# Recurrent attention and a gated FFN on one core: the order of the chunks and the size of the input transfers

## The chip, the cores and the metric

The kernel runs on one core of one Trainium2 chip. The core has a matrix engine (TensorE, PE in the profile), a vector engine (DVE), an activation engine (ACT), GpSimd (POOL) and SyncE (SP), which issues most transfers; 16 DMA engines move data between device memory and the on-chip SBUF. Matrix products are written to eight PSUM banks. The metric is the device time of one execution in microseconds (us).

## The reference

Inputs q, k, v and f_logit are float32 of shape (4 batches, 8 heads, 768 tokens, 48). Each head carries a 48 x 48 state from token to token:

```python
f = 1.0 / (1.0 + np.exp(-f_logit))
for t in range(S):
    state = f[:, :, t, :, None] * state + np.einsum('bhd,bhe->bhde', k[:, :, t], v[:, :, t])
    y[:, :, t] = np.einsum('bhd,bhde->bhe', q[:, :, t], state)
```

The eight heads of a token are then laid side by side to a row x of 384 values, batch after batch (3072 rows), and go through a gated FFN of width 1536:

```python
gate = np.maximum(x @ w_gate, 0.0)
val = x @ w_val
out = gate * val @ w_out
```

## The kernel before

**Chunks.** A batch of 768 tokens is cut into six chunks of 128, called steps (c = 0 to 5). Within a chunk the recurrence is matrix work. With b the running sum of log f, the kernel forms "hats": k times exp(-b) and q times exp(b). Products of hats, masked by a triangle, are the scores; scores times v plus q-hat times the old state is the output y; k-hat times v, added to the old state and scaled by the chunk's whole decay, is the new state. So a chunk of a batch needs the state of the chunk before it in that batch, and different batches do not depend on each other.

**Order.** The kernel goes step by step: step c of all four batches (512 tokens, one group), then step c + 1. The FFN of a group follows once the four chunks of x are there. For steps 0 and 1 the FFN's hidden part is begun in halves of two batches (`groups`).

**One chunk, by engine.** ACT computes exp and ln of the gate (`f_in`, `bneg`). TensorE sums them with a triangular matrix (cum, L715, L718). ACT takes both exponentials (`expo`). GpSimd multiplies them with k and q (`hats`, L737 and L740) and copies v to a padded layout (`vpad`, L772). The hats must be turned round so that the feature lies on partitions (`qkT`): for step 2 on TensorE (L751, copied by DVE in L756), for steps 3 to 5 by a transposing DMA issued on SyncE (L759). TensorE makes the scores (L780), DVE masks them (`ptm`, L785), TensorE makes y, and ACT copies it out. For steps 0 to 2 y is made in transposed form (L807) and copied straight to `xT`; for steps 3 to 5 it is made in natural form (L813, L817), copied to `xn` and turned by a transposing DMA (L832). The state is made by TensorE (L841), DVE (L544: plus old state) and GpSimd (L546: times decay).

**Steps 0 and 1 are loaded otherwise.** `load_duo` puts two neighbouring tokens in one partition (one run of 384 bytes in device memory) and two batches in the two halves of the partitions; `attention_duo` computes both batches of a pair at once from this layout, with its own masks (`seen`, `later`) and sums (`upto`, `below`, `halves`). From step 2 on `load` (L466) brings one step of a pair of batches with one token in a partition: 2048 runs of 192 bytes, 393 KB.

**FFN.** For each of 12 blocks of 128 hidden units `ffn_hidden` makes gate and value (L865, 3 + 3 matmuls of 512 columns), ACT the relu (L871), DVE the product (`gT`, L875). `ffn_out` makes 12 matmuls of 384 columns for each 128 tokens (L888); ACT copies the result (L898), SyncE stores it (L902). The weights are cast to bf16 on the way in, by DMAs issued on GpSimd (L486), in three pieces each (wg, wv, wo).

**The planner.** The whole program is a list of operations with engine, estimated duration, the tiles read and written and a priority. `Plan.schedule` runs a list scheduler over it with these estimates, and so fixes each engine's order of instructions and the PSUM banks; of operations that can start at the same time the one with the lower priority number goes first. At run time each engine works its list in order and waits on semaphores. FFN operations have a priority 1000 higher in number than attention, and `chain` keeps operations of one kind in order. Loads wait until the load `flight` before them has landed. `first` is the order of the first loads; `wg0@q0.1` means that piece 0 of wg waits until that load of q has landed. The planner's model of the DMA queue blocks the issuing engine while more than 3300 descriptors are pending (`CAP`). Until `warm_until` idle gaps of TensorE are filled with matmuls of zeros, and one PSUM bank is kept for them.

Of the kernel before, what the change touches and what calls it, by code (L numbers as in the profile page):

```python
# [93 lines left out]
class Plan:  # L94
# [15 lines left out]
    def link(self):  # L110
        writers, readers = {}, {}
        for op in self.ops:
# [3 lines left out]
            for d in op.follows:  # L116
                deps[d] = "order"
# [167 lines left out]
def bass_hgrn2_outer__then__ffn_reglu_kernel(  # L285
# [25 lines left out]
    GT = B * C  # L311
    assert S % C == 0 and HD == DM == 384 and H == 8 and D == 48 and GT == 512
# [12 lines left out]
    hats = sb("hats", [128, NH, 2, H, 64], BF16)  # L325
    NQ = 8
    qkT = sb("qkT", [128, NQ, 2, NP, C], BF16)
    NM = 4
    ptm_all = sb("ptm", [128, NM, 2, NP, C], BF16)
    ptm = [ptm_all[:, i] for i in range(NM)]  # L330
    NV = 4
    vpad = [sb(f"vpad{i}", [128, VW], BF16) for i in range(NV)]
    st = [[sb(f"st{b}_{i}", [128, SW], BF16) for i in range(2)] for b in range(B)]
    NA = 3
    dec = [sb(f"dec{i}", [128, B, NP, 2], F32) for i in range(NA)]
    NN = 3
    xn = [sb(f"xn{i}", [128, HD], BF16) for i in range(NN)]
    NS = 3
# [8 lines left out]
    NR = 4  # L347
    relu = [sb(f"relu{i}", [128, GT], BF16) for i in range(NR)]
    NO = 4
    osb = [sb(f"osb{i}", [128, DM], F32) for i in range(NO)]  # L350
    tri = sb("tri", [128, C], BF16)
    upto = sb("upto", [128, C], BF16)
    below = sb("below", [128, C], BF16)
    halves = sb("halves", [128, 2], BF16)
    seen = [sb(f"seen{i}", [128, C], BF16) for i in range(2)]
    later = [sb(f"later{i}", [128, C], BF16) for i in range(2)]
# [13 lines left out]
    PE_L = 0.30  # L370

    def act_t(n):
        return dict(occ=0.17 + n / 1150.0, lat=0.2)

    def dve_t(n):
        return dict(occ=0.14 + n / 950.0, lat=0.2)

    def pool_t(n):
        return dict(occ=0.15 + n * 2.2 / 1000.0, lat=0.2)

    def pool_c(n):
        return dict(occ=0.12 + n * 1.05 / 1000.0, lat=0.2)
# [4 lines left out]
    def fill(eng, name, ap, value, cols, prio, key=None):  # L387
        e = engine[eng]
        add(eng, lambda: e.memset(ap, value), [], [key or name], occ=0.1 + cols / 2000.0, prio=prio)

    def triangle(t, name, base, prio, step=-1):
# [46 lines left out]
    def slot_of(n, c, pr):  # L438
        return (2 * c + pr) % NL[n]

# [595 lines left out]
```

## Time and profile before

| | |
|---|---|
| timed runs | 212.6 and 213.74 us, median 213.17 |
| profiled execution, span | 212.9 us; the page shows no time outside it |
| TensorE busy | 193.7 us (91%), mean granted clock 0.984 |
| DVE, ACT, POOL busy | 108.6, 108.7, 81.5 us |
| queue q1 (SyncE's transfers) | 104064 packets, 27.93 MB, 62.4% of 16 engines' span |
| queue q0 (weights, from GpSimd) | 3984 packets, 3.54 MB, 10.1% |
| chain that ended last | PE 66%, DMA 18%, SP's queue 8% |
| issue to landing, median | qkT transpose 4.4 us, xT transpose 3.1 us, weight pieces 8.9 to 10.6 us |

A busy share is a mean over the span; the page also cuts the span into 40 slices of 5.32 us and gives each engine's busy tenths in each. The chain follows the work back from the last instruction, at every step to what released it. In the tables of windows each row is a stretch of the span: its length, busy time of each engine with the number of instructions, the granted TensorE clock, the busy share of the DMA engines (over 1 where packets overlap) and GB/s.

### The profile page before, as it was taken

The numbers are of one execution on the slowest core, as the hardware profiler recorded it, in microseconds if no ns is written. First come the engines' busy times: TensorE is split into PE (matmuls) and PEld (weight loads), VectorE is DVE, ScalarE is ACT, GpSimd is POOL, SyncE is SP. The second block draws the span as 40 slices with busy tenths as digits, with TensorE's granted clock in tenths as the row PEclk, the third lists the DMA queues.
The fourth block names the chain that finished last, engine by engine and source line by source line (L and its number), as shares of the span: only waits on it lengthen the run. The fifth ranks groups of instructions, "written<-read, shape, count | busy, mean of one in ns | idle before, by whom it ended". The sixth has DMA issues, their size and how long they took to land.

```text
span 212.9 us, 4759 instructions
## 1 busy us (share of the span) xinstructions
PE 193.7 (91%) x1929; PEld 109.7 (51%) x1949; DVE 108.6 (51%) x184; ACT 108.7 (51%) x235; POOL 81.5 (38%) x121
## 2 busy tenths in 40 slices
PE   7788599999998999997878999688999999999994
PEld 2265375466776764553433555253555444445562
DVE  7975564582189795664534473253533333233310
ACT  2663167444885878784372654644243344433411
POOL 8939217431795957774515453044000000000000
PEclk9999799999999999999996999999999999999999
DMA  5999999995899899996898995899222100011012
GB/s 125 242 236 220 225 205 220 216 237 121 178 237 210 179 188 189 167 226 133 191 183 183 203 221 125 150 223 150 61 50 64 37 37 37 37 39 38 37 39 109
DMA packets 108069, 31.76 MB, mean 149 GB/s; under 512 B 101136, under 2 KB 108048, under 8 KB 108048
## 3 DMA queue, kind: packets, MB, share of 16 engines
q1 hardware_dynamic: 104064, 27.93, 62.4%
q0 software_dynamic: 3984, 3.54, 10.1%
q8 instruction: 15, 0.25, 0.5%
q14 instruction: 6, 0.05, 0.1%
HBM read 25.95 MB, written 4.72 MB: 144 GB/s over the span
## 4 chain that ended last, share of the span: by engine, by line
PE 66%; DMA 18%; SPq 8%; ACT 2%; POOL 2%; issue 2%; DVE 1%
PE ps L865 37%; PE ps L888 18%; DMA qkT<-hats 5%; DMA wv<-in_moe_w_val_dram 4%; SPq L454 3%; DMA xT<-xn 3%; SPq L832 2%; DMA q_in<-in_q_dram 2%; SPq L759 2%; DMA k_in<-in_k_dram 2%; DMA f_in<-in_f_logit_dram 2%; PE ps L780 2%; PE ps L618 1%; PE ps L715 1%; PE ps L646 1%
## 5 line engine op out<-in xcount | busy, mean ns | idle before, releaser
L875 DVE TENSOR_TENSOR gT<-relu,ps 128x512 bf16<-128x512 bf16 (+1 forms) x82 | 50.2, 620 | 57.9 <-PE ps L865 51.1
L871 ACT ACTIVATE relu<-ps 128x512 bf16<-128x512 f32 (+1 forms) x82 | 44.5, 545 | 37.5 <-PE ps L865 34.3
L865 PE MATMUL ps<-xT,wv 128*128 128x512 bf16 (+1 forms) x243 | 61.1, 361 | 2.3 <-DMA wv<-in_moe_w_val_dram 2.2
L865 PE MATMUL ps<-xT,wg 128*128 128x512 bf16 (+1 forms) x231 | 58.8, 360 | 1.4 <-DMA wg<-in_moe_w_gate_dram 0.4
L888 PE MATMUL ps<-wo,gT 128*128 128x384 bf16 x288 | 51.3, 326 | 0.0
L888 PEld LDWEIGHTS ps<-wo,gT 128*128 128x128 bf16 x288 | 27.1, 98 | 19.2 <-issue 0.2
L865 PEld LDWEIGHTS ps<-xT,wv 128*128 128x128 bf16 x246 | 23.5, 100 | 24.0 <-DMA wv<-in_moe_w_val_dram 2.5
L865 PEld LDWEIGHTS ps<-xT,wg 128*128 128x128 bf16 x246 | 23.1, 100 | 20.4 <-issue 0.8
L898 ACT ACTIVATE osb<-ps 128x384 f32<-128x384 f32 x24 | 11.7, 489 | 34.3 <-PE ps L888 34.2
L785 DVE TENSOR_TENSOR ptm<-ps,tri 128x512 bf16<-128x512 f32 x32 | 21.0, 686 | 13.6 <-PE ps L780 13.5
L737 POOL TENSOR_TENSOR hats<-k_in,expo 128x384 bf16<-128x384 f32 x16 | 15.9, 999 | 22.3 <-DMA k_in<-in_k_dram 14.8
L546 POOL TENSOR_TENSOR st<-ssum,dec 128x384 bf16<-128x384 f32 x16 | 13.2, 828 | 14.1 <-DVE ssum L544 14.1
L740 POOL TENSOR_TENSOR hats<-q_in,expo 128x384 bf16<-128x384 f32 x16 | 15.9, 997 | 4.1 <-DMA q_in<-in_q_dram 4.1
L780 PE MATMUL ps<-qkT 48*128 48x128 bf16 x128 | 6.4, 219 | 6.9 <-DMA qkT<-hats 6.9
L544 DVE TENSOR_TENSOR ssum<-ps,st 128x384 f32<-128x384 f32 x16 | 8.8, 553 | 4.9 <-PE ps L841 4.7
L623 DVE TENSOR_TENSOR ptm<-ps,seen 128x512 bf16<-128x512 f32 x16 | 10.1, 685 | 2.2 <-PE ps L618 2.2
L605 DVE COPY qkT<-ps 128x1024 bf16<-128x1024 bf16 x7 | 4.8, 691 | 10.8 <-PE ps L598 10.7
L945 PE MATMUL ps<-zeros 128*128 128x512 bf16 x30 | 10.0, 481 | 0.1
L706 ACT ACTIVATE f_in<-f_in 128x768 f32<-128x768 f32 x8 | 6.7, 840 | 6.3 <-DMA f_in<-in_f_logit_dram 6.3
L772 POOL CAST vpad<-v_in 128x384 bf16<-128x384 f32 x16 | 7.9, 504 | 4.7 <-DMA v_in<-in_v_dram 4.6
L780 PEld LDWEIGHTS ps<-qkT 48*128 48x128 bf16 x128 | 3.6, 94 | 11.8 <-DMA qkT<-hats 9.5
L725 ACT ACTIVATE expo<-ps 128x384 f32<-128x384 f32 x16 | 7.9, 493 | 2.6 <-PE ps L718 2.5
(90 smaller groups left out, 182.1 us busy)
## 6 DMA issues: line engine op xcount, KB each, us to landing
out_dram<-osb SPq DMA_DIRECT2D x24, 192.0 KB, 2.2
f_in<-in_f_logit_dram SPq DMA_DIRECT2D x8, 384.0 KB, 4.7
k_in<-in_k_dram SPq DMA_DIRECT2D x8, 384.0 KB, 4.5
q_in<-in_q_dram SPq DMA_DIRECT2D x8, 384.0 KB, 5.5
v_in<-in_v_dram SPq DMA_DIRECT2D x8, 384.0 KB, 5.8
f_in<-in_f_logit_dram SPq DMA_DIRECT2D x8, 192.0 KB, 5.0
k_in<-in_k_dram SPq DMA_DIRECT2D x8, 192.0 KB, 6.5
q_in<-in_q_dram SPq DMA_DIRECT2D x8, 192.0 KB, 6.3
```

The source lines that it names most:

```text
L546: add("POOL", lambda: gp.tensor_tensor(t4(s_new), t4(tmp), rate, ALU.mult), [key] + dk, [f"S{b}_{c % 2}"], prio=P + 8, **pool_t(HD))
L623: last_mask[0] = add("DVE", lambda i=i, j=j, s=sj[j]: ve.tensor_tensor(ptm_all[:, m0 + i, j, :, :], s.ap[:, :].rearrange("p (n t) -> p n t ...
L737: add("POOL", lambda: gp.tensor_tensor(hk, kin[:, b % 2, :, :], ex[:, 1, :].rearrange("p (h d) -> p h d", h=H), ALU.mult), in_keys("k", c, ...
L740: add("POOL", lambda: gp.tensor_tensor(hq, qin[:, b % 2, :, :], ex[:, 0, :].rearrange("p (h d) -> p h d", h=H), ALU.mult), in_keys("q", c, ...
L780: mm = te.matmul(s.ap[:, p * C:(p + 1) * C], tokens(c, b, 1, p, lo, lo + D), tokens(c, b, 0, p, lo, lo + D))
L785: add("DVE", lambda j=j, s=s: ve.tensor_tensor(ptm[mi][:, j, :, :], s.ap[:, :].rearrange("p (n t) -> p n t", n=NP), mask, ALU.mult), [s, " ...
L865: mm = te.matmul(bank.ap[:, 0:n], wt[:, kt, j * 128:(j + 1) * 128], xT[xi][:, kt, n0:n1], start=(kt == 0), stop=(kt == NK - 1))
L871: add("ACT", lambda: sc.activation(relu[ri][:, 0:n], gate.ap[:, 0:n], AF.Relu), [gate], [f"relu{ri}"], prio=P, **act_t(n))
L875: add("DVE", lambda: ve.tensor_tensor(gT[gi][:, j, n0:n1], relu[ri][:, 0:n], val.ap[:, 0:n], ALU.mult), [val, f"relu{ri}"], [f"gT{gi}_{j}_ ...
L888: mm = te.matmul(o[b].ap[:, 0:DM], gT[gi][:, j, b * C:(b + 1) * C], wo[:, j, :], start=(j == 0), stop=(j == NJ - 1))
L898: add("ACT", lambda b=b, oi=oi: sc.activation(osb[oi][:, :], o[b].ap[:, 0:DM], AF.Copy), [o[b]], [f"osb{oi}"], prio=P, **act_t(DM))
L945: return te.matmul(spare[:, 0:WARM], zeros[:, 0:128], zeros[:, 0:WARM], start=True, stop=True, skip_group_check=True)
```

## The change

The chunks are taken batch by batch: all six of batch 0, then batch 1, and so on (w = 6b + c). Groups of the FFN are four consecutive chunks in this order, so group 0 holds chunks 0 to 3 of batch 0, group 1 the last two of batch 0 and the first two of batch 1. There is one state at a time. The FFN of every group starts once all four chunks are there.

The two-token layout and its code go. One transfer loads all 768 tokens of a tensor of a batch, 1.18 MB in 6144 runs of 192 bytes, with one token in a partition; two buffers of this size per tensor. In SBUF the runs of k, q and v are 256 bytes apart, those of f 192. `first` loads batch 0 (f0 k0 q0 v0), then weights, then batch 1 behind pieces of the weights (f1 waits for wv2, k1 for wv3). Batches 2 and 3 are loaded by `refill`, each transfer after the tiled or natural product ("intra") of a given chunk. The weights come in four pieces each.

Chunks 0 to 5 turn the hats and x on TensorE (`pe_hats`, `pe_x`), all later chunks by the transposing DMA. In chunks 0 to 5 DVE multiplies k instead of GpSimd. Many buffers are fewer, several estimates of the planner are changed, and `follows` no longer overwrites a stronger dependency.

```diff
             for d in op.follows:
-                deps[d] = "order"
+                deps.setdefault(d, "order")
...
-    duos = (0, 1)
-    pe_hats = {2}
-    x_way = {0: "tiled", 1: "tiled", 2: "tiled", 3: "xbar", 4: "xbar", 5: "xbar"}
-    flight = 3
-    wsteps = 3
-    first = ("f0.0 k0.0 q0.0 f0.1 k0.1 q0.1 v0.0 v0.1 wg0@q0.1 wv0 wg1@v0.1 wv1 wg2 wv2 f1.0 k1.0 q1.0 v1.0 "
-             "wo0@k1.0 wo1@q1.0 wo2 f1.1 k1.1 q1.1 v1.1").split()
+    NW = B * NC
+    GC = 4
+    GT = GC * C
+    wsteps = 4
+    WJ = NJ // wsteps
+    first = 'f0 k0 q0 v0 wg0@k0 wv0@q0 wg1@v0 wv1@v0 wg2@v0 wv2@v0 wg3@v0 wv3@v0 f1@wv2 wo0@wv0 wo1@wv1 k1@wv3 wo2@wv2 wo3@wv3 q1 v1'.split()
+    pe_hats = {0, 1, 2, 3, 4, 5}
+    pe_x = {0, 1, 2, 3, 4, 5}
+    DP = 64
...
-    NL = {"f": 4, "k": 5, "q": 5, "v": 5}
-    ld = {n: sb(f"{n}_in", [128, NL[n], 2, H, D], F32) for n in "fkqv"}
-    NB = 4
+    pitch = {"f": D, "k": DP, "q": DP, "v": DP}
+    ld = {n: [sb(f"{n}_in{i}", [128, H, NC, pitch[n]], F32) for i in range(2)] for n in "fkqv"}
+    NB = 3
-    NE = 4
+    NE = 2
-    NH = 6
+    NH = 5
-    NQ = 8
+    NQ = 6
-    NM = 4
+    NM = 3
-    NN = 3
+    NN = 2
...
+    def load(n, b, c=None, after=()):
+        t, P = ld[n][b % 2], pitch[n]
+        row = H * NC * P
+        flight = 6 if c is not None else 3
+        after = list(after) + sent[-flight:][:1] if len(sent) >= flight else after
+        if c is None:
+            src = bass.AP(tensor=srcs[n].tensor, offset=b * H * S * D, ap=[[D, C], [C * D, H * NC], [1, D]])
+            dst = bass.AP(tensor=t, offset=0, ap=[[row, 128], [P, H * NC], [1, D]])
+            keys, rows, each = [f"{n}{b % 2}_{i}" for i in range(NC)], H * NC * C, 0.012
...
+        op = chain("load", "SP", lambda: sy.dma_start(dst, src), [], keys, occ=0.45, lat=1.2, prio=(b * NC + (c or 0)) * 10 - 40, after=after)
...
+        op = chain("load_w", "POOL", lambda: gp.dma_start(dst, src), [], [f"{nm}{s}"], occ=0.79, lat=1.3, prio=-10, after=after)
...
+    def refill(w):
+        for item in {5: 'f2', 6: 'k2', 7: 'q2', 8: 'v2', 11: 'f3', 12: 'k3', 13: 'q3', 14: 'v3'}.get(w, "").split():
+            load(item[0], int(item[1:]), None, [tails["intra"]])
...
+        for n, x, hv in (("k", 1, hk), ("q", 0, hq)):
+            e = {(0, 'k'): 'DVE', (1, 'k'): 'DVE', (2, 'k'): 'DVE', (3, 'k'): 'DVE', (4, 'k'): 'DVE', (5, 'k'): 'DVE'}.get((w, n), "POOL")
+            add(e, lambda n=n, x=x, hv=hv, e=e: engine[e].tensor_tensor(
+                hv, view(n, b, c, c + 1)[:, 0], ex[:, x, :].rearrange("p (h d) -> p h d", h=H), ALU.mult),
+                [f"{n}{b % 2}_{c}", f"exp{n}{ei}", f"hats{hi}"], [f"h{n}{hi}"], prio=P + 2, **elem_t(e, HD))
...
     pend = []
-    for c in range(NC):
-        if c in duos:
-            for states in [attention_duo(c, pr) for pr in range(B // 2)]:
-                states()
-        else:
-            for b in range(0, B, 2):
-                for n in "fkqv":
-                    loads.append(load(n, c, b, b + 2, loads[-flight:][:1]))
-            for b in range(B):
-                attention_front(c, b)
-                attention(c, b)
-        for b0, b1, js in groups.get(c, [(0, 4, range(NJ))]):
+    for g in range(NW // GC):
+        for r in range(GC):
+            w = g * GC + r
+            if w in {0, 1}:
+                gates(w, 1)
+            elif w % 2 == 0:
+                gates(w, 2)
+            hats_of(w)
+            attention(w)
+            refill(w)
+        for r0, r1, js in {}.get(g, [(0, GC, range(NJ))]):
...
-    warm_until = 17.0
+    warm_until = 20.0
```

More of the change, by code (lines that the diff above doesn't have):

```diff
@@ L811, in natural @@
         def natural():
-            for p in range(NP):
-                te.matmul(y.ap[:, p * 96:(p + 1) * 96], tokens(c, b, 0, p), s_old[:, p * SSTEP:(p + 1) * SSTEP],
-                          start=(p == 0), stop=False, skip_group_check=True)
+            if c:
+                for p in range(NP):
+                    te.matmul(y.ap[:, p * 96:(p + 1) * 96], tokens(w, 0, p), s_old[:, p * SSTEP:(p + 1) * SSTEP],
+                              start=(p == 0), stop=False, skip_group_check=True)
             for h in range(H):
@@ L848, in attention, with state @@
-        if c < NC - 1:
-            rest()
+            op = add("SP", lambda: sy.dma_start(dst, xn[ni][:, :], transpose=True),
+                     [f"xn{ni}"], x_key, prio=P + 8, occ=1.27, lat=0.6)
+            dma(op, f"xT{xi}_{r}", 0.5, 1, 400)
+        if c == NC - 1:
+            return
+        kv = Bank("kv")
+        def state():
+            for p in range(NP):
+                mm = te.matmul(kv.ap[:, p * 96:(p + 1) * 96],
+                               hats[:, hi, 1, 2 * p:2 * p + 2, :].rearrange("p h d -> p (h d)"),
+                               bass.AP(tensor=vp, offset=p * VSTEP, ap=[[VW, 128], [64, 2], [1, D]]))
+            return mm
```

506 lines of the change are left out of this document (143 added, 363 removed).

## The prediction

> **What bounds the kernel now.** I read the page's slices first, then the chain that ended last in order of time, then windows of single stages.
>
> ```profile
> PE   7788599999998999997878999688999999999994
> PEclk9999799999999999999996999999999999999999
> DMA  5999999995899899996898995899222100011012
> GB/s 125 242 236 220 225 205 220 216 237 121 178 237 210 179 188 189 167 226 133 191 183 183 203 221 125 150 223 150 61 50 64 37 37 37 37 39 38 37 39 109
> ```
>
> A slice is 5.32 us. DMA is full to slice 28 (149 us) and then nearly idle, while TensorE is full to the end. So there are three stages: a start until the FFN can begin, a stage to 149 us in which transfers and TensorE run side by side, and 60 us of TensorE alone.
>
> ```profile
> 14.89 9.12 DMA wv<-in_moe_w_val_dram
> 24.05 3.34 PE ps L865 x15
> ...
> 107.59 4.98 DMA qkT<-hats
> ...
> 124.54 5.97 DMA xT<-xn
> ...
> 144.14 5.17 DMA qkT<-hats
> ...
> 180.22 1.95 PE ps L888 x12
> 182.22 3.83 PE ps L865 x17
> ...
> 210.10 0.49 ACT osb L898
> ```
>
> The FFN (L865, L888) runs from 24.05 us; in the middle the chain leaves TensorE for transfers three times.
>
> **The span as a sum.** From the chain's pieces, L888 x12 takes 1.95 us (0.1625 each) and L865 x18 takes 3.88 (0.2156 each). A group of 512 tokens has 72 and 48 of them: 15.5 + 7.8 = 23.3 us; six groups are 140 us. Attention on TensorE, also by the chain's pieces: a two-token step pair costs cum 0.65, totals 0.18, transposes 0.90, scores 2.2, intra 0.73 (with state 1.5), state 0.45; an ordinary chunk costs cum 0.24, scores 0.33, state 0.17, and 0.37 for the natural product or 0.50 for the tiled one, with 0.45 for TensorE transposes. After 24.05 us that is about 32.4 us. The end (copy 0.49, last store 2.3) is 2.8. So 24.05 + 139.6 + 32.4 + 2.8 = 198.9; the other 14 us of the 212.9 us span are waits and slow clock. Nothing is shown outside the span, so I make the sum against 212.9, which lies between the two timed runs (212.6 and 213.74); their median 213.17 is 0.27 higher.
>
> **What goes.** All two-token attention: by the same prices all 24 chunks cost 28.5 us of TensorE instead of about 41. That 12.5 us is a real gain, since TensorE is the bound wherever it does not wait. Fewer constants are built at the start; that is hidden behind the first loads (first GpSimd product only at 9.3 us) and worth nothing.
>
> **Price of a load.** Every load is now 6144 packets of 192 B (1.18 MB).
>
> ```profile
> 8.00:15.00 7.00, 5.22 (x71) 3.28 (x70) 5.92 (x8) 4.55 (x12) 3.30 (x5) 1.00 1.29 238
> 64.00:69.00 5.00, 4.33 (x136) 3.30 (x136) 4.70 (x10) 2.56 (x6) 2.75 (x4) 1.00 1.05 211
> 73.00:74.00 1.00, 1.00 (x34) 0.80 (x30) 1.00 (x3) 1.00 (x3) 0.90 (x2) 1.00 1.27 261
> 100.00:102.00 2.00, 0.77 (x6) 0.38 (x7) 0.92 (x2) 0.00 (x0) 1.58 (x3) 1.00 0.91 181
> 25.00:30.00 5.00, 5.00 (x105) 3.53 (x103) 1.79 (x5) 2.48 (x6) 0.79 (x1) 0.75 1.20 207
> ```
>
> The last number is GB/s. 8 to 15 us is 384-byte packets (238); 64 to 69 is 192-byte loads of 393 KB one behind the other (211); 73 to 74 is the middle of one (261). At 261 a load of 393 KB takes 1.51 us, at 211 it takes 1.86, so each has 0.35 us of edges. The large load has one pair of edges: 1.18 MB / 261 + 0.35 = 4.9 us (bounds 4.4 and 5.6, from 266 GB/s in 36 to 38 us and from 211). A transpose of qkT moves 262 KB at 181 GB/s (100 to 102 us): 1.45 us, one of xT 0.54. A weight piece is 1.8 us: queue q0's 10.1% of the span over 12 pieces.
>
> **The start.** The first load of 768 tokens must land whole before the first exp, where now 128 tokens of two batches land by 5.1 us. First bytes come at 2.5 us; f0 is in SBUF at 2.5 + 4.9 + 0.9 (landing) = 8.2, k0 at 13.1. wg0 is issued then and its bytes come 3.1 us later (as now: issued 13.97, bytes from 17.1), so q0 loses 1.4 us to it and lands at 19.6; v0, which loses the same to wv0, at 26.1. On GpSimd seven weight DMAs (wg1 to wv3, wo0) become ready with v0 at a lower priority number than the casts of v, so I put them ahead: 7 x 0.78 = 5.5 us (nothing, if the planner orders them otherwise), and the casts begin at 31.6. Then the state runs serially through batch 0: cast 0.5, state matmul 0.4, L540 0.55, twice L544 0.55 + L546 0.83, hand-offs about 0.9, intra on a slow clock 0.9, xT copy 0.5: 6.5 us. Group 0 starts at 38.2 instead of 24.05, and whole, where now its first half starts alone: **14 us lost**. The waiting weight DMAs hold up nothing but these casts.
>
> **Group 1 needs batch 1.** f1 waits on SyncE for wv2 (v0 at 26.1, 3.1 to first bytes, four pieces, 1 to land: 37.7), and k1, q1, v1 stand behind it. To 48 us f1 shares with six weight pieces at about 58 GB/s (one load's 393 KB took SyncE 6.65 and 6.85 us then): 0.49 MB; the rest ends at 51.3. k1, q1, v1 end at 56.2, 61.1, 66.0, with landing 66.9. Chunks 6 and 7 have no TensorE transposes: their two qkT stand behind v1 (68.9), f2's 4.9 us can stand before their xT, so xT7 lands at 76, or at 81 if k2 slips in as well; I take 78. TensorE has finished group 0 by 38.2 + 23.3 + 1.7 (slow clock, as 0.75 granted in 25 to 30 us) + 3 (chunks 4, 5) = 66.3, so it waits 12 us, of which the attention of chunks 6 and 7 fills 2. Now, by contrast, no group waits so long.
>
> **The rest.** From 78: five groups 116.5, attention of chunks 8 to 23 16.7 (4.2 + 2 x 6.24), slow clock after the wait 1.7, end 2.8: 215.7. Then waits for later transposes. From first weight bytes (29.2) to xT of chunk 15 the queue must move 18 us of weights (1.3 of it shared), 12 loads 58.8, ten chunks of transposes 20, eight stores 4.4, that is to 129 us; TensorE wants group 3 at about 78 + 56 = 134. So there is slack of 5 us without gaps. The queue's busy share in 45 to 149 us is 0.91 now, which would be 9 us of gaps. Between 0 and 9 I take 4, since SyncE issues in order and a load ahead of a transpose blocks it. Sum: **220 us**. The 18 (12 now) qkT and 18 (12 now) xT transposes on SyncE are in this; ACT, DVE and GpSimd are busy 51%, 51% and 38% and bound nothing after the start. Batch 3's loads (v3 due at about 115 us) end well before chunk 18 is wanted, so the waits that now stand at 107 to 150 us go.
>
> **Rivals.**
> Transfers keep up (2 in 10): f2 and k2 do not pass the transposes of chunks 6 and 7, and later groups wait for nothing. For it: the slack of 5 us. Against it: qkT landing takes 4.4 us median even now, with loads a third as long. Group 1 at 76, then 137.7: 213.7 us, about no change (this kernel's two runs differ by 0.5%; I count 2% as no change).
> Faster (1.5 in 10): large transfers run faster than the rows. It decides when v1 lands by about 60 us instead of 66.9, that is at loads of 4.0 us or less: group 1 then starts at 70, and 137.7 gives 207.7, less what TensorE no longer pays for a cold clock: 206. For it: 261 to 266 GB/s at best moments; against it: no stretch holds it, and packets stay at 192 B. The Trainium skill, "DMA: Bandwidth & Descriptors", section "Rules for kernel authors", asks for 1 MiB or more per DMA, and its section "Bandwidth" gives 341 GB/s for 1 MB; by that a load would take 3.5 us and the start would come at about 33 us, an estimate of 202. No run here shows it yet; the 238 GB/s of loads of 192 KB a piece lies far below that page's table.
> Slower still (1.8 in 10): SyncE's order decides. Each load of 6144 packets stands ahead of an xT that a group waits for, in groups 1, 2 and 3: 81 instead of 78, then 4 to 5 us twice: 228 to 231 us. It decides if TensorE idles over 3 us ahead of groups 2 and 3.
> That the change does not act as told: the large transfer still is 192-byte packets, so it buys only the edges; this is in the forecast.
>
> **Chances.** Forecast 47 in 100 (216 to 226; 7 of the 47 fall within 2%), keep up 20 (16 within 2%, 2 each side), faster 15, slower still 18. So faster by over 2%: 0.17, within 2%: 0.23, slower by over 2%: 0.60. The range 207 to 231 leaves out most of the faster case and the far end of the slower one.
>
> **What would show it.** Right: first L-line of the FFN at 36 to 40 us, f_in landing near 8 us, TensorE idle about 10 us near 66 to 78, no long wait after 150 us, DMA quiet from about 135 us, attention's matmuls gone from 41 to about 28 us. Wrong: the casts of v ahead of the weights (start at 33), loads landing in under 4.4 us, batch 1 in before 60 us, or idle TensorE before several groups.

## The result and the profile after

The changed kernel takes 264.65 us, the median of two runs (264.49 and 264.81), against 213.17: 1.242 times as long (95% interval 1.231 to 1.254). The forecast was 220, with a range of 207 to 231. The sign was right; the loss is 51 us where 7 were expected. The kernel before also has a slower state, so ratios here and below compare fast runs alone; beside e1_nogap, e2_late and e3_nogap_late these took 208.1 and 209.4 us.

First the slices of the changed kernel's page (one slice is 6.58 us), with the same four rows as were shown of the kernel before:

```profile
PE   8451759999922840398689595999999999999995
PEclk9975755999985555579959898899999999999999
DMA  6999999999998978988699888962200220000012
GB/s 141 178 163 190 138 149 202 253 185 166 164 195 188 227 140 152 161 136 187 111 177 160 152 153 162 204 75 62 60 32 32 75 75 32 31 30 30 32 60 90
```

DMA is full for 26 slices (to 171 us), where before it was full for 28 shorter ones (149 us). TensorE has a hole from 72 to 112 us (the digits 2, 2, 8, 4, 0, 3), and from 79 us the granted clock lies at half. GB/s is 140 to 200 for most of the way; before it was mostly 180 to 240.

The chain that ended last, in order of time (start, length, what). It answers to the six pieces that were shown of before, where the chain reached the FFN at 24.05 us (its first matmul ran at 21.4) and left TensorE three times in the middle:

```profile
14.29 17.13 DMA v_in<-in_v_dram
...
35.58 9.02 DMA wv<-in_moe_w_val_dram
...
66.98 14.62 DMA f_in<-in_f_logit_dram
81.62 0.84 ACT f_in L494
...
91.94 8.68 DMA k_in<-in_k_dram
100.62 8.87 DMA xT<-xn
109.53 1.46 PE ps L660 x3
...
130.27 9.54 DMA qkT<-hats
...
150.14 9.86 DMA v_in<-in_v_dram
```

Here L660 is the FFN's hidden product and L683 its output product (L865 and L888 before). The chain is on transfers for most of the time until 109.5 us, and leaves TensorE twice more for about 10 us each. Around these two stretches TensorE itself stands still only 2.1 us (until 131 us), 3.1 (until 149) and 3.1 (until 161); the rest of the time it has other work.

**One sum for all kernels below.** The span is TensorE's busy time at full clock, plus what the slow clock adds, plus its idle time. "At full clock" is busy time times granted clock, added up over stretches of 5 us; the slow clock's share is busy time less that. Busy time includes the matmuls of zeros at the start, about 10 us in both kernels here. All three in us:

| profiled execution | span | work at full clock | slow clock | idle |
|---|---|---|---|---|
| before | 212.9 | 191.1 | 2.7 | 19.2 |
| after | 263.1 | 182.6 | 21.9 | 58.6 |
| difference | +50.2 | -8.5 | +19.2 | +39.4 |

So attention's saving on TensorE is there. It is outweighed by waits (39.4 us more idle time), and the slow clock adds about half as much (19.2).

### The profile page after: what moved, and what is told of

It is laid out like the page before. It is cut to its first block, busy times and chain, and to the rows that moved or that the text cites. A ratio compares the mean times of both kernels' runs of the same rounds, so it can differ in the third digit from the quotient of the medians.

```text
span 263.1 us, 3915 instructions
## 1 busy us (share of the span) xinstructions
PE 204.5 (78%) x1535; PEld 107.3 (41%) x1535; DVE 98.3 (37%) x162; ACT 109.8 (42%) x235; POOL 80.2 (30%) x110
## 4 chain that ended last, share of the span: by engine, by line
PE 44%; DMA 31%; SPq 15%; POOL 3%; issue 3%; ACT 2%; DVE 1%; POOLq 0%
PE ps L660 25%; SPq L440 14%; PE ps L683 14%; DMA v_in<-in_v_dram 10%; DMA f_in<-in_f_logit_dram 6%; DMA xT<-xn 5%; DMA qkT<-hats 4%; DMA wv<-in_moe_w_val_dram 3%; DMA k_in<-in_k_dram 3%; PE ps L568 2%; SPq L620 1%; PE ps L605 1%; POOL st L643 1%; POOL wg L457 1%; PE ps L629 1%
## 5 line engine op out<-in xcount | busy, mean ns | idle before, releaser
L670 DVE TENSOR_TENSOR gT<-relu,ps 128x512 bf16<-128x512 bf16 x72 | 49.4, 687 | 92.1 <-PE ps L660 80.0
L660 PE MATMUL ps<-xT,wg 128*128 128x512 bf16 x216 | 62.3, 400 | 16.6 <-DMA xT<-xn 14.0
L660 PE MATMUL ps<-xT,wv 128*128 128x512 bf16 x216 | 62.0, 398 | 0.0
L666 ACT ACTIVATE relu<-ps 128x512 bf16<-128x512 f32 x72 | 42.9, 597 | 41.5 <-PE ps L660 41.2
L683 PE MATMUL ps<-wo,gT 128*128 128x384 bf16 x288 | 52.3, 330 | 0.0
L660 PEld LDWEIGHTS ps<-xT,wg 128*128 128x128 bf16 x216 | 21.0, 101 | 41.3 <-DMA xT<-xn 14.1
L573 DVE TENSOR_TENSOR ptm<-ps,tri 128x512 bf16<-128x512 f32 x48 | 30.6, 684 | 18.3 <-PE ps L568 17.1
L683 PEld LDWEIGHTS ps<-wo,gT 128*128 128x128 bf16 x288 | 27.7, 99 | 20.3 <-issue 1.5
L660 PEld LDWEIGHTS ps<-xT,wv 128*128 128x128 bf16 x216 | 20.8, 101 | 24.7 <-issue 3.2
L529 POOL TENSOR_TENSOR hats<-q_in,expo 128x384 bf16<-128x384 f32 x24 | 23.6, 1000 | 8.5 <-DMA q_in<-in_q_dram 7.3
L694 ACT ACTIVATE osb<-ps 128x384 f32<-128x384 f32 x24 | 11.8, 491 | 31.9 <-PE ps L683 31.8
L516 ACT ACTIVATE expo<-ps 128x384 f32<-128x384 f32 x24 | 11.8, 491 | 15.1 <-POOL hats L529 9.7
L507 PE MATMUL ps<-bneg,tri 128*128 128x384 bf16 x24 | 9.4, 403 | 9.2 <-ACT bneg L495 9.2
L518 ACT ACTIVATE expo<-ps 128x384 f32<-128x384 f32 x24 | 11.6, 494 | 11.5 <-POOL hats L529 11.5
L494 ACT ACTIVATE f_in<-f_in 128x768 f32<-128x768 f32 (+1 forms) x13 | 10.0, 788 | 14.2 <-DMA f_in<-in_f_logit_dram 14.2
L618 ACT ACTIVATE xn<-ps 128x384 bf16<-128x384 f32 x18 | 8.7, 490 | 15.5 <-DMA xT<-xn 12.0
## 6 DMA issues: line engine op xcount, KB each, us to landing
k_in<-in_k_dram SPq DMA_DIRECT2D x4, 0.2 KB, 12.3
```

Of the source, the lines that this page charges most:

```text
L516: add("ACT", lambda: sc.activation(ex[:, 1, :], bc.ap[:, 0:HD], AF.Exp, scale=1.0), [bc], [f"expk{ei}"], prio=P + 1, **act_t(HD))
L518: add("ACT", lambda: sc.activation(ex[:, 0, :], bc.ap[:, 0:HD], AF.Exp, scale=-1.0), [bc], [f"expq{ei}"], prio=P + 1, **act_t(HD))
L529: add(e, lambda n=n, x=x, hv=hv, e=e: engine[e].tensor_tensor(hv, view(n, b, c, c + 1)[:, 0], ex[:, x, :].rearrange("p (h d) -> p h d", h= ...
L573: add("DVE", lambda j=j, s=s: ve.tensor_tensor(ptm[mi][:, j, :, :], s.ap[:, :].rearrange("p (n t) -> p n t", n=NP), mask, ALU.mult), [s, " ...
L660: mm = te.matmul(bank.ap[:, 0:n], wt[:, kt, j * 128:(j + 1) * 128], xT[xi][:, kt, n0:n1], start=(kt == 0), stop=(kt == NK - 1))
L666: add("ACT", lambda: sc.activation(relu[ri][:, 0:n], gate.ap[:, 0:n], AF.Relu), [gate], [f"relu{ri}"], prio=P, **act_t(n))
```

## The experiments

The time of the kernel before lay between 211.8 and 212.2 us (medians) beside these runs.

### The price of a load: the distance between runs in SBUF

A load's rate is worked out from the start times of its packets: the middle 80% of its bytes over the time they took. In the changed kernel the four f loads run at 179 to 238 GB/s (the slowest beside weight transfers), all twelve of k, q and v at 165 to 181. All of them are 6144 runs of 192 bytes. What differs is `pitch`: f's runs touch in SBUF, those of k, q and v lie 256 bytes apart.

**e1_nogap** takes the gap away:

```diff
-    DP = 64
+    DP = 48
```

> One thing is undone: the runs of k, q and v lie 192 bytes apart in SBUF, without the gap of 64 bytes, as those of f do. Order, sizes and waits stay. Theory A (the gap makes these twelve transfers slow, and everything behind them in the queues is late): k, q and v come to the rate of f, 230 to 240 GB/s in their middle instead of 165 to 180, 5.2 to 5.5 us each instead of 7.1; the FFN starts near 40 us instead of 45.3, group 1 near 94 instead of 109.5, the whole takes 240 to 248 us. Theory B (the gap is innocent, k, q and v are slow because they stand in a queue of large transfers): rates stay at 165 to 180 GB/s and the time within 2% of 264.7.

Measured: 247.6 us (246.92 to 248.99), ratio 1.187 (1.177 to 1.198). The same two windows of both kernels, the first within f0, the second within k0 (length; busy time and count of PE, PEld, DVE, ACT, POOL; clock; DMA share; GB/s). The kernel after:

```profile
3.00:7.50 4.50, 4.10 (x14) 1.44 (x12) 0.91 (x2) 0.00 (x0) 3.08 (x6) 1.00 1.04 234
9.00:13.00 4.00, 2.44 (x17) 1.20 (x18) 0.00 (x0) 3.81 (x10) 0.00 (x0) 0.90 1.08 177
```

Without the gap:

```profile
3.00:7.50 4.50, 3.91 (x14) 1.38 (x12) 0.91 (x2) 0.00 (x0) 3.08 (x6) 1.00 1.04 233
9.00:13.00 4.00, 2.66 (x17) 1.30 (x18) 0.00 (x0) 3.98 (x11) 0.00 (x0) 0.85 1.06 232
```

In the last column k0 goes from 177 to 232 GB/s, and the DMA share is over 1 either way: a "full" queue says nothing of what it moves. The time lies in theory A's range; the FFN starts at 41.6 us, and group 1's first relu comes at 99.1 instead of 111.0.

The packets themselves are not what was forecast. The changed kernel's page has for SyncE's queue (packets, MB, share of 16 engines' span):

```profile
q1 hardware_dynamic: 54784, 30.09, 59.3%
```

Sixteen loads of 6144 packets would be 98304 by themselves. In the trace each whole load is 1536 packets of 768 bytes, four runs to a packet, with the gap and without it. So neither the packet's size nor its number explains the two rates.

**e4_swap** exchanges the two layouts, to see whether it is the tensor or the place:

```diff
-    pitch = {"f": D, "k": DP, "q": DP, "v": DP}
+    pitch = {"f": DP, "k": D, "q": D, "v": D}
```

> The gap is moved: f gets runs 256 bytes apart, k, q and v have them 192 bytes apart. If the distance between the runs in SBUF sets the rate, f falls to 165 to 180 GB/s and k, q and v rise to 225 to 240. If it is the tensor or its place in the order, the rates stay with the names.

Measured: 253.49 us (one run); f now runs at 175 to 180 GB/s (f1, beside weight transfers, at 144) and k, q, v at 218 to 240. The first window, within f0, of this kernel:

```profile
3.00:7.50 4.50, 3.52 (x14) 1.27 (x12) 0.91 (x2) 0.00 (x0) 3.08 (x6) 1.00 1.07 178
```

It is the distance. **e9_pitches** asks which distance, with f 192, k 208, q 224 and v 240 bytes:

```diff
-    pitch = {"f": D, "k": DP, "q": DP, "v": DP}
+    pitch = {"f": D, "k": 52, "q": 56, "v": 60}
```

> The changed kernel with four distances between the 192-byte runs in SBUF: f 192 bytes (as it is), k 208, q 224, v 240 instead of 256 for all three. A look at the rate of each tensor's loads, first to last packet, not at the sum. Theory A (any gap costs, since runs that touch are merged to longer packets): f 230 to 240 GB/s, k, q and v all 165 to 185. Theory B (the distance of 256 bytes costs, as a pattern of banks or lines): k, q and v at other distances run near 230 GB/s. Theory C (the rate falls with the distance): k about 220, q about 205, v about 190. Time 247 to 266 us accordingly.

Measured: 253.93 us (one run). Loads that share the queue with no weights ran at 225 to 236 GB/s (f), 206 to 210 (k), 205 to 217 (q) and 195 to 212 (v). None of the three theories holds as written. In these whole loads a gap of 16 to 48 bytes costs about a tenth, whichever it is, and 256 bytes costs about a quarter. Why 256 is worse is open.

### SyncE's order: loads ahead of transposes

SyncE's own timeline of the changed kernel (start, length, issue) shows what stood ahead of group 1. qkT and xT are the crossbar transposes of chunks 6, 7 and later; `xT` of chunk 7 is the one at 100.62:

```profile
66.98 6.55 SPq L440 DMA_DIRECT2D f_in<-in_f_logit_dram  x1
73.58 6.65 SPq L697 DMA_DIRECT2D out_dram<-osb  x1
80.28 4.10 SPq L547 DMA_TRANSPOSE qkT<-hats  x3
...
90.21 1.26 SPq L620 DMA_TRANSPOSE xT<-xn  x1
91.94 0.72 SPq L440 DMA_DIRECT2D k_in<-in_k_dram  x1
93.11 7.45 SPq L440 DMA_DIRECT2D q_in<-in_q_dram  x1
100.62 6.72 SPq L620 DMA_TRANSPOSE xT<-xn  x1
```

Behind a load in flight, one issue holds SyncE 6.55 to 7.45 us in this stretch, a store (73.58) as much as a load. f2 and a store stand ahead of the first transposes, k2 and q2 ahead of the last. So group 1 waits for three loads that only group 3 needs. The chain above shows a second wait for f2 in the same stretch: until 81.62 us ACT waits for it, and behind that exponential TensorE has a sum of batch 2 ahead of the scores of chunk 6. What SyncE's order costs by itself is seen in e14_pe_only below.

**e2_late** puts the refill behind the transposes instead of the products:

```diff
-        for item in {5: 'f2', 6: 'k2', 7: 'q2', 8: 'v2', 11: 'f3', 12: 'k3', 13: 'q3', 14: 'v3'}.get(w, "").split():
-            load(item[0], int(item[1:]), None, [tails["intra"]])
+        for item in {11: 'f2 k2 q2 v2', 15: 'f3 k3 q3 v3'}.get(w, "").split():
+            load(item[0], int(item[1:]), None, [tails["turned"]])
```

Here `tails["turned"]` is the xT transpose of that chunk.

> Only the order is changed: the loads of batch 2 wait until x of chunk 11 has been turned by its transfer, those of batch 3 until that of chunk 15, so that no load stands ahead of the transposes of chunks 6 to 11. The gap of 64 bytes stays. Theory C (SyncE's order: loads issued ahead of transposes hold up group 1): group 1 starts at 82 to 88 us instead of 109.5 and the whole takes 228 to 242 us. Theory A alone (only the speed of the loads matters): group 1 may start earlier, but the same bytes must pass, and the time stays above 255.

Measured: 249.17 us (248.54 to 250.02), ratio 1.194 (1.182 to 1.207). Group 1's first relu comes at 89.9 us instead of 111.0, near theory C's 82 to 88. The time misses that theory's range, since part is given back. The chain of this kernel, in order of time:

```profile
88.82 1.95 PE ps L661 x5
...
107.69 17.14 DMA v_in<-in_v_dram
...
143.16 14.23 DMA k_in<-in_k_dram
```

Batches 2 and 3 now arrive late: TensorE stands still 6.6 us for v2 (until 125.5 us) and 4.5 us for v3 (until 172.4). Group 3 starts 29.4 us earlier than in the changed kernel (151.5 instead of 180.9), but group 4 only 15.8 (190.6 instead of 206.4): what is given back is lost ahead of group 4, on batch 3.

**e3_nogap_late** has both edits.

> Both edits, no gap and late loads of batches 2 and 3. If A and C are both causes and little else is: FFN from 40 us, group 1 from 75 to 79, and the sum of the prediction then gives 76 + 137.7 to 79 + 137.7 plus 2 to 6 us of waits: 214 to 223 us. If a third cause of size remains, above 228.

Measured: 232.56 us (230.5 to 233.62), ratio 1.113 (1.098 to 1.128). The two edits save 17.0 and 15.5 alone and 32.1 together. That is above 228, so by what was written beforehand there is a third cause.

**e5_truth** asks why the planner put the loads there. It counts 0.012 us for a run of a whole load:

```diff
-            keys, rows, each = [f"{n}{b % 2}_{i}" for i in range(NC)], H * NC * C, 0.012
+            keys, rows, each = [f"{n}{b % 2}_{i}" for i in range(NC)], H * NC * C, 0.0135 if P == D else 0.0185
```

> The changed kernel with one thing altered: the planner that fixes SyncE's order counts 0.012 us for each 192-byte run of a whole load, and here it counts 0.0135 for the contiguous tensor and 0.0185 for the three that land 256 bytes apart, as the trace of the changed kernel has it (5.4 and 7.2 us a load). The gap itself stays. Theory A (the order of SyncE is wrong because the planner counts the loads too short): the planner now puts the transposes of chunks 6 and 7 ahead of f2, k2 and q2, group 1 starts at 90 to 95 us instead of 109.5, as where the refill was put later by hand, and the time is 245 to 253 us. Theory B (the order follows from the priorities, in which a load of batch 2 stands ahead of work of chunk 7, not from the price): the order stays nearly as it is and the time is 260 to 268 us.

Measured: 257.76 us (256.91 to 258.22), between the two theories. f2 still stands ahead of the transposes of chunk 6, but q2 now stands behind the xT transposes. The right price gains 7 us, about half of what moving the refill gains in e2_late (15.5).

**e14_pe_only** undoes one part of the change, the crossbar, and nothing else:

```diff
-    pe_hats = {0, 1, 2, 3, 4, 5}
-    pe_x = {0, 1, 2, 3, 4, 5}
+    pe_hats = set(range(NW))
+    pe_x = set(range(NW))
```

> The changed kernel with its gap and its refill as they are, and only the 36 crossbar transposes on TensorE instead. It undoes one part of the change by itself. Theory A (group 1 starts at 109.5 us because the transposes of chunks 6 and 7 stand behind f2, a store, k2 and q2 on SyncE): now no transpose stands there, group 1 starts at 85 to 92 us when q1 and v1 are in and chunks 6 and 7 are through, and the time is 264.65 less 20 plus up to 10.4 of TensorE: 244 to 256 us. Rival (group 1 waits for the loads as such, not for SyncE's order): group 1 starts at 104 us or later and the time is 262 to 275 us.

Measured: 264.55 us (263.35 to 265.63), the time of the changed kernel to 0.1 us. Yet group 1's first relu comes at 84.1 us instead of 111.0, so theory A is right on what held group 1: f2 lands at 81.6 us as before, and with the transposes off SyncE group 1 no longer waits for what follows it there. Its time, 244 to 256 us, is missed: all 27 us are given back before group 3, which starts at 180.6 us (180.9 in the changed kernel). The chain shows part of it:

```profile
99.80 13.90 DMA f_in<-in_f_logit_dram
113.72 1.58 ACT f_in L494 x2
...
121.84 14.47 DMA v_in<-in_v_dram
```

ACT works its list in order too. It waits until 113.72 us for f3, which only group 4 needs, and relus and exponentials stand behind. How much of the 27 us goes that way was not tested. An equal time does not mean that an edit did nothing.

### The rest of 20 us: two causes that hide one another

Six runs without the gap, e6_chunks to e13_pe, tried to find the third cause by small edits. **e6_chunks** is e3_nogap_late with batch 0 in 24 loads of one chunk:

```diff
-    first = 'f0 k0 q0 v0 wg0@k0 wv0@q0 wg1@v0 wv1@v0 ...'.split()
+    first = ('f0.0 k0.0 q0.0 v0.0 f0.1 k0.1 q0.1 v0.1 f0.2 f0.3 k0.2 q0.2 v0.2 ... '
+             'wg0@q0.1 wv0@v0.1 wg1@v0.3 wv1@v0.3 ...').split()
```

> The kernel without the gap and with the later refill (232.56 us), and batch 0 now in 24 loads of one chunk each instead of four whole loads; batches 1 to 3 stay whole. Theory A (the rest of the loss at the start is the wait for whole transfers): chunk 0's four tensors are in by about 8 us, the first weight piece is issued at about 9, the FFN starts at 30 to 34 instead of 41 us, and the time falls by 5 to 10, to 222 to 228 us. Rival (batch 1 sets group 1 whatever happens at the start, and later waits for batch 2 and 3 set the end): the FFN starts earlier, TensorE then waits longer ahead of group 1, and the time stays within 3 us of 232.6.

Measured: 233.66 us (231.63 to 235.39). The FFN starts at 31.9 instead of 41.1 us, and group 1 at 83.9 instead of 83.1. The rival holds: the nine microseconds turn into a longer wait for group 1.

**e12_refill** only spreads the refill (no gap):

```diff
+        for item in {7: 'f2', 8: 'k2', 9: 'q2', 10: 'v2', 13: 'f3', 14: 'k3', 15: 'q3', 16: 'v3'}.get(w, "").split():
+            load(item[0], int(item[1:]), None, [tails["turned"]])
```

> The changed kernel without the gap, and with the refill spread: f2, k2, q2 and v2 each behind the xT transpose of chunks 7, 8, 9 and 10, f3 to v3 behind those of chunks 13 to 16. (With all of batch 2 behind chunk 11 and all of batch 3 behind chunk 15 it was 232.56 us, with TensorE idle 3 us each near 110 and 150 us and a cold clock behind the waits.) Theory A (the rest of the loss is batches 2 and 3 that come late because they were refilled late): no wait over 3 us after group 1 has begun, and 220 to 227 us. Rival (the rest lies ahead of group 1, at 82 us, and cannot be had back by the refill): 229 to 235 us.

Measured: 234.8 us (233.67 to 236.36); the rival holds. **e11_spaced** adds the start in chunks, and puts all weight pieces but the first two behind casts of v on GpSimd (`prio=45` instead of -10).

> The same spread refill without the gap, and in addition batch 0 in loads of one chunk and the later weight pieces behind the first casts of v on GpSimd. Theory A (what was lost ahead of the FFN is part of what is left): 5 to 9 us below the run with the spread refill alone, that is 212 to 220 us, the FFN from 28 to 32 us. Rival (batch 1 must be whole before group 1 whatever the start does, 13 MB of loads and weights at some 200 GB/s: 65 us): within 3 us of that run, with a longer wait ahead of group 1.

Measured: 234.92 us (233.53 to 235.71), with the FFN from 30.2 us and group 1 at 84.5 us. The rival again.

**e10_stream** loads every batch by chunk (96 loads of 196 KB, each pair of chunks behind the pair that frees its buffer; transposes by crossbar as in the change):

```diff
+        if w % 2 and w + 12 < NW:
+            b, c = divmod(w - 1 + 12, NC)
+            for n, i in (('f', 0), ('f', 1), ('k', 0), ('q', 0), ('v', 0), ('k', 1), ('q', 1), ('v', 1)):
+                load(n, b, c + i, [tails.get("turned", tails["intra"])])
```

> The changed kernel without the gap, and every batch in loads of one chunk each (96 loads of 196 KB instead of 16 of 1.18 MB); a pair of chunks is loaded again as soon as the pair that used its buffer has gone through its own transposes. All attention is the changed kernel's. Theory A (the whole transfer is what is left of the loss: what waits for a chunk waits for a batch, and what SyncE issues behind a load waits for 6144 rows): the FFN starts at 30 to 34 us, no wait of group 1 over 5 us, and the time is 203 to 216 us, that is the kernel before or better by part of the 12.5 us that attention saves on TensorE. Rival (the transposes by crossbar and the loads together are too much for the queue, whatever the size of a load): 224 to 236 us, with TensorE still waiting for xT and qkT between 80 and 150 us.

Measured: 232.61 us (232.31 to 234.71), ratio 1.103 (1.091 to 1.114); the rival. **e17_stream_truth** is the same with the planner told 0.0145 instead of 0.0178 us for a run of a chunk load.

> No gap, every batch in loads of one chunk, transposes by crossbar from chunk 6 on as in the change, and the planner told 0.0145 instead of 0.0178 us for a run of a chunk load (0.93 us a load instead of 1.14, as contiguous loads ran at 211 to 235 GB/s). Theory A (the planner's price spoils TensorE's order: sums of chunks 8 to 11 ahead of the scores of 6 and 7): 218 to 226 us, group 1 ahead of 78 us. Rival (the order hardly depends on that price, the crossbar's hand-offs do): 229 to 236 us.

Measured: 233.3 us (232.71 to 234.29). Group 1's first relu comes 5 us earlier (83.0 instead of 88.1) and the time is the same; the price is not it.

**e13_pe** takes e12_refill and puts all transposes on TensorE (`pe_hats` and `pe_x` as in e14_pe_only, the refill behind the products).

> The spread refill without the gap, and all 36 crossbar transposes on TensorE instead (with their copies on DVE and ACT), so that SyncE issues only loads and stores. On TensorE that adds 18 x (0.45 + 0.13) = 10.4 us by the rows of the kernel before. Theory A (the transposes on SyncE and in the queue, each behind loads and behind one another, are what is left): idle TensorE and cold clock fall by more than is added, and the time is 214 to 222 us. Rival (the crossbar no longer costs TensorE anything once the refill is in order): the added work comes on top, 232 to 242 us.

Measured: 233.87 us (232.88 to 233.97). The time lies in the rival's range, though not for its reason: the crossbar did cost. Group 1 starts 9.3 us earlier (74.9 instead of 84.2). The work at full clock is 12.3 us more (192.8 instead of 180.5), idle time 8.3 and the slow clock 6.4 less: they nearly cancel.

So loads by chunk alone gave about 2 us, and transposes on TensorE alone about 1. **e15_pe_stream** does both (with the refill behind the products, since no xT transpose is left):

> No gap, every batch in loads of one chunk, and all transposes on TensorE: the start in chunks and the crossbar taken out together. Theory A (two causes hide one another: an early start is taken back by group 1 behind the crossbar, and an early group 1 is no gain while the start is late): the FFN from 30 to 32 us, group 1's first ReLU at 58 to 66 us, and 214 to 222 us. Rival B (the order by batches costs the rest, since one batch's chunks follow one another through state, hats and masks where the kernel before has four batches side by side): group 1 at 72 us or later, 228 to 236 us.

Measured: 219.27 us (218.47 to 220.68), ratio 1.036 (1.028 to 1.045). The time and the FFN's start are theory A's; group 1's first relu, at 68.9 us, lies between the two theories. The four kernels without the gap side by side ("FFN" and "group 1": first hidden product of the FFN, first relu of group 1):

| loads | transposes from chunk 6 on | us | FFN | group 1 | work | slow clock | idle |
|---|---|---|---|---|---|---|---|
| whole (e12_refill) | crossbar | 234.8 | 41.3 | 84.2 | 180.5 | 15.0 | 39.1 |
| by chunk (e10_stream) | crossbar | 232.6 | 31.3 | 88.1 | 184.5 | 12.6 | 33.8 |
| whole (e13_pe) | TensorE | 233.9 | 41.1 | 74.9 | 192.8 | 8.6 | 30.8 |
| by chunk (e15_pe_stream) | TensorE | 219.3 | 31.9 | 68.9 | 193.9 | 5.5 | 17.9 |

The two kernels with loads by chunk run 11 to 13 more matmuls of zeros at the start, some 3 us of their work. With the crossbar an early start runs into a group 1 that begins at 83 to 88 us in all these runs. With whole loads an early group 1 buys little: from group 1 to group 3 e13_pe takes 75.3 us and e15_pe_stream 60.9. Loads by chunk are not only smaller but asked for earlier (chunks 12 and 13 behind chunk 1, a whole f2 behind chunk 7); which of the two counts is not separated. e10_stream's chain shows how group 1 is held although chunks 6 and 7 were loaded by then:

```profile
60.40 1.37 SPq L551
...
62.44 3.41 DMA k_in<-in_k_dram
...
74.28 3.22 DMA qkT<-hats
```

Between 60 and 86 us this chain goes through k of a later chunk, GpSimd's hats, masks and a crossbar transpose, with TensorE's granted clock at 0.55. The same stretch, 50 to 75 us, of e10_stream and then of e15_pe_stream (columns as in the windows above):

```profile
50.00:75.00 25.00, 14.77 (x154) 8.78 (x151) 6.24 (x11) 13.78 (x34) 11.87 (x15) 0.75 0.81 160
```

```profile
50.00:75.00 25.00, 21.90 (x274) 13.30 (x273) 12.07 (x21) 12.91 (x32) 11.25 (x14) 0.86 1.00 208
```

TensorE goes from 14.8 to 21.9 us busy of 25.

**e16_pe_start** is the control: all transposes on TensorE, batch 0 by chunk, batches 1 to 3 whole.

> As the run before, but only batch 0 is loaded by chunk (with the later weights behind the first casts of v); batches 1 to 3 are whole loads with the spread refill. Theory A: batch 1 is in at 62 to 66 us whatever the start does, group 1 at 72 to 76 us, so the early start is lost again and the time is 228 to 235 us; the whole load of batch 1 is then what the chunk loads of the other run save. Rival (it is the crossbar alone that took the early start back): 214 to 224 us, like the other run.

Measured: 238.27 us (237.9 to 239.07), and group 1 at 75.8 us: v1's last packet starts at 66.4 us. Theory A, a little beyond its range. It is batch 1 (and later ones) in whole loads that wastes the early start: from group 1 to group 3 this kernel takes 78.3 us. A start in chunks by itself is worth nothing.

### Where the crossbar may stay, and what the gap is worth then

**e19_pe12** and **e20_pe18** are e15_pe_stream with chunks 12 to 23, or 18 to 23, back on the crossbar (`pe_hats = pe_x = set(range(12))`, or 18).

> The run with no gap, loads by chunk and all transposes on TensorE (219.27 us), with chunks 12 to 23 back on the crossbar (24 transposes on SyncE, none before about 85 us). TensorE does 12 x 0.58 = 7 us less. Theory A (the crossbar hurt only in group 1, where nothing covers its latency): 211 to 216 us. Rival (24 transposes between 80 and 150 us still stand behind loads and cost waits, as in the kernel before): 218 to 226 us.

> As the run before, with only batch 3's chunks 18 to 23 on the crossbar (12 transposes, when few loads are left). TensorE does 6 x 0.58 = 3.5 us less than with all on TensorE. Theory A: 214 to 217 us. Rival (any crossbar transposes cost as much as they save): 218 to 222 us.

Measured: 227.71 us (225.12 to 228.44) and 215.07 us (214.44 to 217.07), ratio 1.019 (1.007 to 1.031). The first is the rival's, a little beyond its range, the second theory A's. The last six chunks on the crossbar save 4.2 us, just the 4.0 us of work that leaves TensorE (193.9 to 189.9). The six before them cost 12.6. The window from 117 to 134 us of e19_pe12, and then of e20_pe18 (columns as in the windows above):

```profile
117.00:134.00 17.00, 6.96 (x103) 4.58 (x99) 5.58 (x10) 9.86 (x25) 9.49 (x12) 0.71 0.94 177
```

```profile
117.00:134.00 17.00, 16.82 (x133) 8.94 (x135) 7.61 (x13) 12.25 (x31) 10.40 (x13) 1.00 0.90 190
```

With the crossbar TensorE waits ten of these seventeen microseconds and its clock falls, in a queue that is as full in both. In e20_pe18 SyncE issues the last load at 135.15 us and five of the six qkT transposes between 139 and 148: behind the loads, not among them. This is the fastest version found in the new order, 3 us behind the kernel before; none beat it.

**e21_gap_back** puts the gap back into e15_pe_stream (`DP = 64`).

> The run with loads by chunk and all transposes on TensorE (219.27 us), with the gap put back: k, q and v land 256 bytes apart again. Theory A (the gap slows every load, whatever its size and whatever stands behind it): 72 loads of k, q and v at about 1.14 instead of 0.85 us, 20 us more of queue, of which the part up to batch 1 is on the path: 227 to 238 us. Rival (a queue that no transposes wait for has the room): 217 to 223 us.

Measured: 220.51 us (219.82 to 221.37). The rival holds, and this qualifies the first experiment. In a load by chunk the runs lie 1536 bytes apart with the gap and 1152 without. The packets do take longer with it; queue q1 in the two pages, without and with the gap (packets, MB, share of 16 engines' span):

```profile
q1 hardware_dynamic: 103296, 23.60, 51.9%
```

```profile
q1 hardware_dynamic: 103296, 23.60, 64.5%
```

The same bytes take a quarter more of the engines' time, but the medians differ by only 1.2 us, and the ranges of the two kernels' runs overlap. The padding that cost 17 us costs about 1 where no transpose waits behind loads and nothing waits for a whole batch; which of these two conditions matters more was not tested.

## Why the prediction was wrong

By its own steps:

- **What bounds the kernel, and the span as a sum: right as a reading.** The 14 us left over as "waits and slow clock" after 24.05 us fit the trace: in all, 19.2 us of idle and 2.7 of slow clock, of which some 9 us of idle are the start and the end.
- **What goes (12.5 us of TensorE): right in kind, too large.** The work at full clock fell by 8.5 us. Added up by tiles, attention's part of it goes from about 39 to about 30 us, where 41 and 28.5 were forecast.
- **Price of a load (4.9, bounds 4.4 to 5.6): the first step that failed.** f0 took 5.5 us, within the bounds; k, q and v took 6.9 to 7.9 (7.3 in the mean), well outside. The rows of before only had loads whose runs touch in SBUF. The gap of `DP = 64`, told of in the change, was priced at nothing; e1_nogap and e4_swap show that it is a quarter of the rate, worth 17 us here. Without it the loads took 5.2 to 6.3 us (5.8 in the mean, f1 beside weights left out): 261 GB/s was one microsecond's rate and not that of a load, so about 0.9 us of the error is not the gap's. The "6144 packets of 192 B" were 1536 of 768. e21_gap_back, where the same padding costs about 1 us, shows that most of the 17 lies in what stood behind the loads or waited for a whole one.
- **The start: right in its parts, 7 us late, 5.3 of them by the loads.** The casts waited 5.4 us for weight DMAs on GpSimd (5.5 predicted), and the serial chain after them took 8.1 us (6.5). v0 was in at 31.4 instead of 26.1, so the FFN began at 45.25 instead of 38.2.
- **Group 1 from 78: the step that failed most.** It began at 109.5. v1's last packet came at 74.7 (66.9 predicted for its landing), by the loads' price. From there the working had 11 us with f2 ahead of the transposes, or 14 if k2 slipped in. It took 35 us: f2 held SyncE for 6.55 us, a store for 6.65, q2 for 7.45, and the last xT itself for 6.72. Moving only the refill brings group 1 back to 89.9 us (e2_late); taking only the transposes off SyncE, to 84.1 (e14_pe_only).
- **The rest (137.7 and 4 of waits): 153.6.** Waits went on, 9.5 and 9.9 us in the chain at 130 and 150. From 109.5 to 187 us TensorE was idle for 11.2 us and lost 8 to the slow clock. The slack of 5 us of queue had been worked out with loads of 4.9 us; the twelve loads took 85.6 us from first to last packet instead of 58.8, which by itself turns the slack into a lack of some 22 us.
- **The slow clock (1.7 twice): 21.9 us.** It was priced as two short episodes. Added up over stretches of 5 us, 8.2 us fall ahead of 50 us, 5.9 between 70 and 110, and 7.8 after that. How much of each is on the path to the end was not tested. The granted clock is 0.50 in all of 81 to 109.5 us, with TensorE at work for 10.2 of the 28.5 us, and 0.88 in the stretch behind it:

```profile
81.00:109.50 28.50, 10.20 (x140) 7.54 (x140) 8.42 (x14) 10.38 (x24) 9.57 (x12) 0.50 0.89 171
109.50:187.00 77.50, 66.29 (x511) 32.59 (x512) 37.10 (x60) 35.70 (x79) 31.27 (x40) 0.88 0.79 141
```

- **The rivals.** "Slower still" named the right mechanism, SyncE's order, with its test (TensorE idle over 3 us ahead of groups 2 and 3); the waits came (2.1 us ahead of group 2, 3.1 twice ahead of group 3), and group 1's was far longer than all of them, but it was priced at 8 to 11 us, each load at 4.9 and one or two of them in the way. "Faster" and "keep up" fall. By the Trainium skill ("DMA: Bandwidth & Descriptors", "Bandwidth") a 1 MB transfer moves 341 GB/s; no load here, at 1.18 MB, passed 240, with runs of 192 bytes. The same row gives that transfer 6.15 us, which divided out is about 170 GB/s, so the row alone does not support the 3.5 us that the forecast took from it; the loads here took 5.2 us and more. Nor did the 238 GB/s of 192 KB loads lie far below that table: it has no row for this size, and 238 lies between its 138 for 64 KB and its 341 for 1 MB. What the forecast called certain, that the large transfer still is packets of 192 bytes, did not hold: they were of 768 bytes. What it took from that, that little is gained, did: no load passed the 261 GB/s of the rows of before.

Two errors multiplied: a load of k, q or v was half again as long as counted, and more of them stood in order ahead of the work. Undoing both brings back 32 of the 51 us (e3_nogap_late); loads by chunk with transposes on TensorE bring the kernel to 219.3 us, all but 6 of the 51. Of the 43 us between 220 and the span of 263.1, 31.5 are there when group 1 begins, the rest come after.

Still open: why runs 256 bytes apart are slower than those at 208 to 240; how much of the 3 us that e20_pe18 keeps is the start (FFN at 32.2 instead of 21.4) and how much the order by batches.

## What to carry to other kernels

Price a transfer by both ends, the runs in device memory and their spacing where they land, and then ask what the issuing engine has behind it: a slow load costs little by itself and a great deal when transposes, stores and a whole batch's work stand behind it in order. When single mends leave the time where it is, compare where each stage starts before calling them useless: two causes can hide one another, and only both together show (234.8, 232.6 and 233.9, but 219.3). Split the span into work at full clock, slow clock and idle; a kernel that saves work can lose twice over by waiting.

## What the runs showed of the hardware that was not expected

- Whole loads of 192-byte runs, without weight transfers beside them, moved 218 to 240 GB/s where the runs touch in SBUF, 195 to 217 where they are 208 to 240 bytes apart, and 162 to 182 at 256 bytes, whatever the tensor. With loads by chunk SyncE's queue took 51.9% of the engines' time where all runs lie 1152 bytes apart, and 64.5% for the same bytes where those of k, q and v lie 1536 apart.
- In the changed kernel, behind a load in flight, an issue held SyncE for about as long as a load takes: a load up to 7.45 us, a store of 192 KB 6.65, an xT transpose 6.72.
- The granted clock fell to 0.50 and stayed there for 28 us while TensorE worked about a third of the time; in the table of four kernels the slow clock's share follows the idle time, from 5.5 us beside 17.9 to 15.0 beside 39.1.
